# Around the last segment: unpaced loads, Gelus behind the last exponential, and a new order of the tail

## The chip, the cores and the metric

The kernel runs on one core of a Trainium2 chip. The metric is the device time of one execution in microseconds (us), as the median of several runs. The profile is one execution, taken by the hardware profiler; its times count from the start of its span.

## The reference

The reference is one transformer block over 2048 tokens of width 512. The attention part goes through the sequence in 64 segments of 32 tokens, one after the other, because 8 memory rows are handed from each segment to the next. The MLP part follows for all tokens.

```
mem = mem0                                   # 8 rows
for s in range(64):                          # x is layernormed first
    h = concat([mem, x[32 s : 32 s + 32]])   # 40 rows x 512
    q, k, v = h Wq, h Wk, h Wv               # 32 heads of 128
    p = softmax(mask(q k^T * 128**-0.5))
    o = (p v) Wo                             # 40 rows x 512
    mem = o[:8]; outs.append(o[8:])
h  = x + concat(outs)
h2 = h + gelu(layernorm(layernorm(h)) w1 + b1) w2 + b2    # 512 -> 1792 -> 512, tanh Gelu
```

## The kernel before, in words

**How the work is staged.** Of the eight rows that a segment hands on, the next segment needs the result at once; everything else of a segment may lag. The kernel therefore runs a chain of segments in which the tensor engine (PE) projects q, k and v for 24 own rows and 8 memory rows, multiplies scores and values for the memory rows, and applies Wo (`wo`, L1294). The ordinary rows' softmax (`sa_mm`, L1182, with the exponential at L1209) and their values (`pv_a`, L1236; its result leaves PSUM in `pv_a_ev`, L1257) follow one segment later. The last eight rows of each segment are handled for blocks of four segments, that is for 128 tokens, by `wo_B` (L1321) and `fold` (L1347), which queues its small adds on POOL. `nat` (L1354) turns a finished block of 128 output rows back by a transposing DMA (L1356), adds x (L1359), takes the layernorm statistics and writes the rows to `h_mid` in HBM (L1376).

**The MLP.** It works in four groups of 512 tokens. Group 0 is treated apart. Its w1 product is done during segments 56 to 63 in places where PE would have had gaps: `hx_early` (L1461) loads a block of `h_mid` into one of the buffers kq 4 and 5, VectorE (DVE) normalizes it in place (L1465), `hn_early` (L1468) transposes it by DMA, `w1_early` (L1454) loads slices of w1 and `w1_pair` (L1480) multiplies two of the 14 column blocks of w1 at a time (L1488). The products of the first six pairs are copied out of PSUM without Gelu into homes in buffers that are no longer used (`gT0_home`). ScalarE (ACT) holds the exponential's table until the last softmax, so that the Gelus of group 0 (`gelu`, L1473; its instructions are L1476) come at the end. The seventh pair is multiplied behind the last segment; its two Gelus read PSUM directly and are the first to run. The order in which group 0's w2 products (L1681) use the 14 blocks is `ORDER0` (L32): 12, 13, 0, 1, ... 11. The list `rest` (L1708) says which other work is put in front of which w2 step: `nat` of block 14, `pv_a` of segment 63, `wo_B` of block 15 with its folds, `wo` of "segment" 65 (the ordinary rows of segment 63) and `nat` of block 15. `wo(NS, ...)` (L1705) is the same for segment 62. The last four w2 steps run tile by tile (L1732), and DVE adds the residual out of PSUM (L1735) and the result is stored (L1737).

Groups 1 to 3 load their rows from `h_mid` (`p2_load`, L1420), normalize them on DVE (`p2_norm`, L1426), transpose them by DMA (`p2_T`, L1437), add b2 to the residual on POOL (`p2_res`, L1432), and then run w1 (L1674), Gelu (L1677) and w2 (L1681) with a lag of four blocks. The row buffer and the residual buffer have two halves; group 2 takes group 0's half, and so its load waits for `p2_res(0)`. The w2 loads (L1692, seven of 256 KB) and w1 loads (L1697, eight of 224 KB) go into the memory of Wk and are free to start when the last segment's k projection is done.

**What sets the order.** All operations are recorded with their data dependencies and planned durations, and PE's order is written out by hand (`ORDERS`, `ORDER_LAST`). `schedule` (L260) is a list scheduler: it takes operations by a key from `PLAN` or by their rank (the longest planned way to the end), and puts each at the earliest free place on its engine; where an operation may run on ACT or DVE (`either`, L206) it goes where it would end first. `lat` (L241) is the planned delay from one operation to a dependent one: 2.0 us behind a DMA, with exceptions. Each engine then runs its operations in that order and waits on semaphores; all DMAs of this part go through one in-order queue on the SP engine.

**Pacing.** PE's instructions are fetched in blocks of 256 (`FETCH_N`) by DMA. `windows` (L404) goes through the SP queue after planning, and from segment 2 on moves each DMA to a stretch between two planned fetches, by making it wait for a PE operation:

```
i = bisect.bisect_right(ends, t) - 1
o.start = max(t, ends[i])
if pe[i] not in o.deps:
    o.deps.append(pe[i])
```

Then `order` (L436) sorts every queue by start, so a DMA that was moved also gets a later place in the SP queue. The other engines' planned starts are not worked out again. `pads` and `pauses` shift PE's fetch points and add waits on PE near them.

Of the kernel before, what the change touches and what calls it, by code (L numbers as in the profile page):

```python
# [17 lines left out]
HOP = {"pe": 0.23, "act": 0.04, "dve": 0.04, "pool": 0.06, "sp": 2.0}  # L18
# [10 lines left out]
KEEP = True  # L29
WINDOWS, WIN_LO, WIN_HI, WIN_BEHIND = True, 1.0, -0.8, 0.4  # L30
PAUSES, PAUSE_IN, PAUSE_US = 3, 64, 0.5
ORDER0 = (12, 13, 0, 1, 2, 3, 4, 5, 6, 7, 8, 9, 10, 11)  # L32
HALVES = ("kq", "KA", "QT", "ZCm", "VS", "nmc", "EC", "rsc", "PC", "PTC", "OTm", "OTx", "KB", "QTB", "VSB", "W1o")
BONUS = {'TTS': -3.0, 'opB': -3.0, 'TTB': -3.0}
LEAN = 0.2
# [116 lines left out]
class Sched:  # L152
# [87 lines left out]
    @staticmethod  # L240
    def lat(p, o):  # L241
        if p.is_dma:
            return {"oN": 4.4, "xT": 3.6}.get(p.kind, HOP["sp"])
        if p.eng == "pe" and o.eng == "pe":
            return 0.0
        return HOP[p.eng] + (0.06 if o.eng == "pe" else 0.0)
# [157 lines left out]
    def windows(self):  # L404

        self.align()
        pe = self.streams["pe"]
        ends = [o.start + o.dur for o in pe]
        t0 = min(o.start for o in pe if o.tag is not None and o.tag[0] == 2)
        marks = [t for t, _ in self.marks if t > t0] + [1e9]  # L410
        used = [t + d for t, d in self.marks if t > t0] + [1e9]
        for o in self.streams["sp"]:
            early = o.start
            for d in o.deps:
                early = max(early, d.start + d.dur + self.lat(d, o))
            o.start = early
            if not o.is_dma or o.start < t0:
                continue
            late = min([d.start - o.dur - self.lat(o, d) for d in o.succ], default=1e9)
            size = o.span  # L420
            w = max(0, bisect.bisect_right(marks, early) - 1)
            while w < len(marks) - 1:
                t = max(early, used[w])
                if t + size <= marks[w + 1] + WIN_HI or t > late:
                    break
                w += 1
            if w >= len(marks) - 1 or t > late:
                continue
            used[w] = t + size
# [4 lines that stand above are left out]
        self.order()  # L434
# [212 lines left out]
ACTF = mybir.ActivationFunctionType  # L647
# [17 lines left out]
FC = F // P  # L665
NTOK = 2048
NS = NTOK // SEG
NTB = NTOK // P
# [48 lines left out]
def build_kernel(nc, A_x, A_mem0, A_Wq, A_Wk, A_Wv, A_Wo, B_w1, B_b1, B_w2, B_b2, out):  # L717
    scale = float(E) ** -0.5
    S = Sched(nc)
    st = contextlib.ExitStack()  # L720
    with st:
# [14 lines left out]
        xT = XX[:, 2, :].rearrange("p (c t) -> p c t", c=DC)  # L736
        hB = XX[:, 3, :].rearrange("p (b c t) -> p b c t", b=RBLK, c=DC)
        oN = sb("oN", [P, DC, P])
# [20 lines left out]
        EC = sb("EC", [P, 2, 64], F32)  # L759
# [3 lines left out]
        SA = sb("SA", [P, 8, LK], F32)  # L763
# [22 lines left out]
        b1t = sb("b1t", [P, FC], F32)  # L786
# [32 lines left out]
        for j in range(4):  # L819
            for b in range(2):  # L820
# [5 lines left out]
             reads=["maskL"], writes=["maskL"])  # L826
# [143 lines left out]
        def copy2(out, src, n, ps_=True, scale_=None):  # L970

            fast = 1.0 if ps_ else 0.5
            if scale_ is None:
                return {"act": (lambda e: e.copy(out, src), t_act(n, ps_)), "dve": (lambda e: e.tensor_copy(out, src), 0.155 + 1.0e-3 * n * fast)}  # L974
            return {"act": (lambda e: e.mul(out, src, scale_), t_act(n, ps_)),  # L975
                    "dve": (lambda e: e.tensor_scalar(out, src, scale_, None, ALU.mult), 0.155 + 1.0e-3 * n * fast)}
# [280 lines left out]
        def pv_a_ev(s):  # L1257
            bk, sg = s // 4, s % 4
            two, keys = pv_a_place(s)
            for t in range(2):  # L1260
                src = two[:, t, :].rearrange("p (k q) -> p k q", q=SEG)[:, :, 0:NA]
                S.either(copy2(OT[:, s % 2, 16 * t:16 * t + 16, 0:NA], src, 384), reads=[keys[t]], writes=[("OTx", s % 2, t)])
            src = two.rearrange("p t (k q) -> p t k q", q=SEG)[:, :, :, NA:SEG]
            ot = OTB[:, bk % 2, :, 8 * sg:8 * sg + 8].rearrange("p (t k) q -> p t k q", t=2)
            S.either(copy2(ot, src, 256), reads=keys, writes=[("OTB", bk % 2, sg)])
# [81 lines left out]
        def fold(n, after=()):  # L1347
            tag, S.tag = S.tag, None
            for f in folds[:n]:
                S.narrow(f(after))  # L1350
            del folds[:n]
            S.tag = tag
# [39 lines left out]
        SBT = TBS * P  # L1392
# [77 lines left out]
            S.dma(lambda e: e.dma_start_transpose(hnT0[:, :, t, :], kq[:, i].rearrange("p a e b -> p (a e b)")), 256, reads=[("kq", i)],  # L1470
                  writes=[("hnT", "first", t)] + hnT0_keys[t], after=after)

        def gelu(fc, src, reads, first):  # L1473
            p = fc // 2
            g = gT0_home[p][0][:, fc % 2, :]
            S.op("act", lambda e: e.activation(g, g if src is None else src, ACTF.Gelu_apprx_tanh, bias=b1t[:, fc:fc + 1], scale=1.0),  # L1476
                 reads=[("gT0", fc), "b1t"] + reads, writes=[("gT0", fc)] + (gT0_home[p][1] if reads else []), dur=0.65 + 1.1 * first,
                 after=[S.last_writer["SA"], S.last_writer[("EC", 1)]] + ([] if first else [S.last_writer[("gT0", ORDER0[0])]]))

        def w1_pair(p, banks, keep=True):  # L1480
            views, keys = homes[p]
            for cc in range(DC):
                v, c0, _ = [w for w in views if w[1] <= cc < w[2]][0]

                def f(e, v=v, c=cc - c0, cc=cc):
                    for n in range(2):
                        for j in range(4):
                            ins = e.matmul(ps[banks[n]][32 * j:32 * j + 32, 0:SBT], v[:, c, n * P + 32 * j:n * P + 32 * j + 32], hnT0[:, cc], start=(cc == 0), stop=(cc == DC - 1),  # L1488
                                           tile_position=(0, 32 * j), skip_group_check=True)
                    return ins  # L1490
                S.op("pe", f, reads=keys + [("W1p", p, c) for c in range(DC)] + [("hnT", "first", t) for t in range(TBS)], writes=[("ps", b) for b in banks],
                     dur=0.4315, mode=MC, ni=16)
            g, gkeys = gT0_home[p]
            for n in range(2):
                if keep:
                    S.either(copy2(g[:, n, :], ps[banks[n]][:, 0:SBT], SBT), reads=[("ps", banks[n])], writes=[("W1o", n), ("gT0", 2 * p + n)] + gkeys)
                else:
                    gelu(2 * p + n, ps[banks[n]][:, 0:SBT], [("ps", banks[n])], n == 0)

        def gT_of(k, fc):  # L1500
            return gT0_home[fc // 2][0][:, fc % 2, :] if k == 0 else gT[:, fc, :]
# [199 lines left out]
        p2_T(1)  # L1701

        early, later = (5, 6), 4
        w1_pair(NP - 1, early, False)
        wo(NS, later, mem=False)  # L1705
        for fc in range(FC - 2):
            gelu(fc, None, [], False)
        rest = {0: lambda: nat(NTB - 2), 3: lambda: (pv_a(NS - 1), pv_a_ev(NS - 1)), 5: lambda: (wo_B(NTB - 1, later), fold(14)), 7: lambda: (wo(NS + 1, 7, mem=False), nat(NTB - 1))}  # L1708
        p2_res(0)
        for n, fc in enumerate(ORDER0[:FC - 4]):  # L1710
            rest.get(n, lambda: None)()
# [82 lines left out]
```

## Time and profile before

| what | value |
| --- | --- |
| median of 3 runs | 803.06 us |
| the runs | 800.70, 804.13, 803.06 us |
| the profiled execution's own time | 802.49 us |
| its span | 800.8 us |
| mean granted PE clock in it | 0.994 |
| PE busy | 766.7 us |
| last segment's projections on PE end | about 692.8 us |
| group 0's w2 products start | 702.1 us |
| group 1's w1 products start | 722.5 us |

The profile is read as follows. PE, PEld, DVE, ACT, POOL and SPq are the matmuls, the weight loads, VectorE, ScalarE, GpSimd and the DMA queue of SP. A row of a timeline gives the start, the duration, the engine, the source line, the operation with its output and input buffers, the count, and in brackets the idle time of the engine before it with what ended that. MLP buffers lie in the memory of attention buffers and are shown under those names: WK is w1 and w2, WQ holds group 1 to 3's Gelu results and rows, WV the normalized rows, the residual and the output.

### The profile page before, as it was taken

What the parts mean: (1) busy time and instruction counts of PE and PEld (TensorE: products, weight loads), DVE (VectorE), ACT (ScalarE), POOL (GpSimd) and SP (SyncE); (2) the same over time, 40 slices, a digit from 0 to 9 for tenths busy, and PEclk for the clock granted to TensorE, in tenths of its full rate; (3) what the DMA queues carried; (4) which work ended last, traced back from release to release, by engine and by line L of the source; (5) the groups of instructions that cost most, each with busy time, mean ns of one, the idle gap of its engine ahead of it and who ended that gap; (6) DMA issues with size and microseconds to landing.
All of it is one profiled execution on the core that took longest, in us unless ns stands there. A gap on an engine that the chain in (4) does not pass through costs nothing.

```text
span 800.8 us, 45344 instructions
## 1 busy us (share of the span) xinstructions
PE 766.7 (96%) x19686; PEld 424.6 (53%) x20409; DVE 583.3 (73%) x1859; ACT 530.6 (66%) x1381; POOL 308.5 (39%) x831
## 2 busy tenths in 40 slices
PE   3789999999999999999999999999999999989998
PEld 1345455555655555555555555565655666533443
DVE  3258788888888888888888888888888787722211
ACT  2447777777677777677777777777676767643432
POOL 3013223434343444444444444444452425364300
PEclk9999999999999999999999999999999999999999
DMA  9950001010102010201010101010113101275200
GB/s 334 395 180 24 17 14 26 18 45 14 44 7 57 4 48 13 47 14 43 18 43 18 41 21 42 18 37 23 37 31 83 50 25 49 70 185 131 80 26 27
DMA packets 65056, 48.02 MB, mean 60 GB/s; under 512 B 28500, under 2 KB 61276, under 8 KB 64860
## 3 DMA queue, kind: packets, MB, share of 16 engines
q1 hardware_dynamic: 64528, 44.85, 19.5%
q8 instruction: 158, 2.59, 1.3%
q14 instruction: 38, 0.31, 0.1%
q10 hardware_dynamic: 332, 0.27, 0.1%
HBM read 31.08 MB, written 8.13 MB: 49 GB/s over the span
## 4 chain that ended last, share of the span: by engine, by line
PE 92%; DMA 3%; SPq 2%; ACT 2%; issue 1%; DVE 0%; DVEq 0%; ACTq 0%
PE high L956 34%; PE high L699 17%; PE quad L1286 15%; PE quad L1681 5%; PE high L1674 5%; PE high L1325 3%; SPq L859 2%; PE quad L1139 2%; DMA WQ<-in_A_Wq_dram 2%; PE quad L1196 2%; PE quad L1246 2%; PE high L1488 2%; PE quad L1170 1%; PE high L1170 1%; PE high L1286 1%
## 5 line engine op out<-in xcount | busy, mean ns | idle before, releaser
L956 PE MATMUL high<-WQ,hT 128*32 128x512 bf16 x1796 | 158.1, 383 | 1.3 <-DVE hT L1292 1.0
L699 PE MATMUL high<-WK,hT 128*32 128x512 bf16 x1260 | 127.0, 379 | 0.1
L1219 POOL TENSOR_TENSOR PA<-SA,rsa 128x256 bf16<-128x256 f32 x64 | 39.7, 620 | 219.6 <-DVE rsa L1211 131.1
L1286 PE MATMUL quad<-WO,OT 128*32 128x256 bf16 x4032 | 122.5, 273 | 0.7 <-issue 0.7
L956 PE MATMUL high<-WV,hT 128*32 128x512 bf16 x1528 | 115.7, 379 | 0.0
L975 ACT ACTIVATE kq<-high 128x512 bf16<-128x512 f32 x160 | 94.2, 598 | 22.0 <-PE high L956 18.6
L974 ACT CAST kq<-high 128x512 bf16<-128x512 f32 x161 | 93.8, 583 | 21.7 <-PE high L956 20.0
L1286 PEld LDWEIGHTS quad<-WO,OT 128*32 128x32 bf16 x4032 | 102.1, 97 | 6.4 <-issue 1.4
L1227 POOL COPY BD<-PTA 32x128 f32<-32x128 f32 x256 | 78.6, 307 | 16.3 <-DVE PTA L1223 0.6
L956 PEld LDWEIGHTS high<-WQ,hT 128*32 128x32 bf16 x1796 | 52.4, 95 | 56.0 <-issue 24.0
L997 DVE STREAM_TRANSPOSE KALL<-kq 128x256 f32<-128x256 f32 x160 | 69.4, 434 | 9.7 <-ACT kq L974 7.0
L974 ACT CAST VS<-high 128x512 bf16<-128x512 f32 x126 | 73.2, 581 | 0.1
L954 PEld LDWEIGHTS <-hT 128*32 128x32 bf16 x3248 | 52.6, 96 | 35.4 <-DVE hT L1292 7.9
L1677 ACT ACTIVATE WQ<-high,b1t 128x512 bf16<-128x512 f32 x42 | 28.9, 687 | 55.8 <-PE high L1674 55.8
L974 ACT CAST OT<-quad 128x384 bf16<-128x384 f32 (+1 forms) x126 | 47.3, 375 | 24.3 <-PE quad L1174 23.2
L1298 DVE STREAM_TRANSPOSE TT<-quad 128x256 f32<-128x256 f32 x63 | 28.4, 450 | 42.7 <-PE quad L1286 42.5
L1033 ACT COPY KALL<-KALL 128x128 f32<-128x128 f32 x63 | 18.8, 298 | 59.2 <-PE quad L1196 59.0
L997 DVE STREAM_TRANSPOSE QT<-kq 128x256 f32<-128x256 f32 x128 | 54.5, 426 | 1.6 <-ACT kq L975 1.3
L956 PE MATMUL high<-WK,hT 128*32 128x512 bf16 x788 | 55.2, 379 | 0.0
L1338 POOL TENSOR_TENSOR opT<-TTB,TTS 32x64 bf16<-32x64 f32 x128 | 40.3, 315 | 35.9 <-DVE opT L1292 20.0
L699 PE MATMUL high<-WV,hT 128*32 128x512 bf16 x520 | 53.2, 379 | 0.0
L1139 PEld LDWEIGHTS quad<-KALL,ZC 128*32 128x32 bf16 x1984 | 31.0, 96 | 41.6 <-POOL BD L1227 17.8
(187 smaller groups left out, 1612.0 us busy)
## 6 DMA issues: line engine op xcount, KB each, us to landing
WV<-in_A_Wv_dram SPq DMA_DIRECT2D x4, 1024.0 KB, 10.2
WK<-in_A_Wk_dram SPq DMA_DIRECT2D x4, 1024.0 KB, 18.6
WQ<-in_A_Wq_dram SPq DMA_DIRECT2D x4, 1024.0 KB, 17.6
WO<-in_A_Wo_dram SPq DMA_DIRECT2D x16, 256.0 KB, 7.5
v_last<-VSB SPq DMA_DIRECT2D x60, 64.0 KB, 2.4
VBD<-v_last SPq DMA_DIRECT2D x60, 64.0 KB, 2.0
h_mid<-xr SPq DMA_DIRECT2D x16, 128.0 KB, 1.9
WQ<-h_mid SPq DMA_DIRECT2D x4, 512.0 KB, 4.5
```

What stands on the lines that cost most here:

```text
L699: return e.add_instruction(mybir.InstMatmult(name="I-%d" % (4000000 + _kept[0]), engine=mybir.EngineType.PE, start_tensor_calc=start, stop ...
L954: e.ldweights(l, tile_position=(0, 32 * j))
L956: ins = e.matmul(o, l, m, start=(k == 0), stop=(k == DC - 1), tile_position=(0, 32 * j), skip_group_check=True)
L974: return {"act": (lambda e: e.copy(out, src), t_act(n, ps_)), "dve": (lambda e: e.tensor_copy(out, src), 0.155 + 1.0e-3 * n * fast)}
L975: return {"act": (lambda e: e.mul(out, src, scale_), t_act(n, ps_)), "dve": (lambda e: e.tensor_scalar(out, src, scale_, None, ALU.mult), ...
L997: S.op("dve", lambda e: e.transpose(out, src), reads=[("kq", i)], writes=[key], dur=t_dve(256) + 0.02)
L1139: ins = e.matmul(o[32 * j:32 * j + 32, :], zc_window(h), rhs, start=False, stop=(i == 3), tile_position=(0, 32 * j), skip_group_check=True)
L1227: S.narrow(S.op("pool", lambda e, j=j, rows=rows: e.tensor_copy(words(BD[rows, par, :, j, :, :]), words(PTA[rows, 0:4])), reads=["PTA"], w ...
L1286: ins = e.matmul(ps[bank][32 * j:32 * j + 32, 0:256], lhs(slot(h)), wo_cols(h, b), start=(k == 0), stop=(k == 15), tile_position=(0, 32 * ...
L1338: return e.tensor_tensor(o[32 * q:32 * q + 32, c:c + 2], x, y, ALU.add)
L1674: ins = e.matmul(ps[bank][:, 0:SBT], W1[:, cc, fc * P:(fc + 1) * P], hnT_of(k)[:, cc, :], start=(cc == 0), stop=(cc == DC - 1))
L1681: S.op("pe", lambda e: e.matmul(quad[:, t, c0:c0 + w], gT_of(k, fc)[:, t * P:(t + 1) * P], W2[:, fc, c0:c0 + w], start=(fc == (0 if k else ...
```

## The change

Five edits are made. `windows` leaves DMAs alone whose planned start lies at or behind the first PE operation of the last segment (`t1`). The planned latency behind the early row loads into kq 4 and kq 5 is 4.0 us, not 2.0. The seventh w1 pair is copied out of PSUM like the others, on ACT or DVE, and all 14 Gelus run in place, in the order 0 to 13; each waits for the last exponentials, and all but the first also for the first. `ORDER0`, and with it the order of the w2 loads and products, is 0 to 13. In the tail, the Gelus are recorded ahead of `wo(NS, ...)`, and three of the entries of `rest` come two w2 steps earlier.

```diff
-ORDER0 = (12, 13, 0, 1, 2, 3, 4, 5, 6, 7, 8, 9, 10, 11)
+ORDER0 = tuple(range(14))
...
         if p.is_dma:
-            return {"oN": 4.4, "xT": 3.6}.get(p.kind, HOP["sp"])
+            return {"oN": 4.4, "xT": 3.6, "kq4": 4.0, "kq5": 4.0}.get(p.kind, HOP["sp"])
...
         t0 = min(o.start for o in pe if o.tag is not None and o.tag[0] == 2)
+        t1 = min(o.start for o in pe if o.tag is not None and o.tag[0] == NS - 1)
...
-            if not o.is_dma or o.start < t0:
+            if not o.is_dma or not t0 <= o.start < t1:
                 continue
...
-        def gelu(fc, src, reads, first):
-            p = fc // 2
-            g = gT0_home[p][0][:, fc % 2, :]
-            S.op("act", lambda e: e.activation(g, g if src is None else src, ACTF.Gelu_apprx_tanh, bias=b1t[:, fc:fc + 1], scale=1.0),
-                 reads=[("gT0", fc), "b1t"] + reads, writes=[("gT0", fc)] + (gT0_home[p][1] if reads else []), dur=0.65 + 1.1 * first,
-                 after=[S.last_writer["SA"], S.last_writer[("EC", 1)]] + ([] if first else [S.last_writer[("gT0", ORDER0[0])]]))
-
-        def w1_pair(p, banks, keep=True):
+        def gelu(fc):
+            g = gT0_home[fc // 2][0][:, fc % 2, :]
+            S.op("act", lambda e: e.activation(g, g, ACTF.Gelu_apprx_tanh, bias=b1t[:, fc:fc + 1], scale=1.0), reads=[("gT0", fc), "b1t"], writes=[("gT0", fc)],
+                 dur=0.65 + 1.1 * (fc == 0), after=[S.last_writer["SA"], S.last_writer[("EC", 1)]] + ([S.last_writer[("gT0", 0)]] if fc else []))
+
+        def w1_pair(p, banks):
...
             for n in range(2):
-                if keep:
-                    S.either(copy2(g[:, n, :], ps[banks[n]][:, 0:SBT], SBT), reads=[("ps", banks[n])], writes=[("W1o", n), ("gT0", 2 * p + n)] + gkeys)
-                else:
-                    gelu(2 * p + n, ps[banks[n]][:, 0:SBT], [("ps", banks[n])], n == 0)
+                S.either(copy2(g[:, n, :], ps[banks[n]][:, 0:SBT], SBT), reads=[("ps", banks[n])], writes=[("W1o", n), ("gT0", 2 * p + n)] + gkeys)
...
         early, later = (5, 6), 4
-        w1_pair(NP - 1, early, False)
+        w1_pair(NP - 1, early)
+        for fc in range(FC):
+            gelu(fc)
         wo(NS, later, mem=False)
-        for fc in range(FC - 2):
-            gelu(fc, None, [], False)
-        rest = {0: lambda: nat(NTB - 2), 3: lambda: (pv_a(NS - 1), pv_a_ev(NS - 1)), 5: lambda: (wo_B(NTB - 1, later), fold(14)), 7: lambda: (wo(NS + 1, 7, mem=False), nat(NTB - 1))}
+        rest = {0: lambda: nat(NTB - 2), 1: lambda: (pv_a(NS - 1), pv_a_ev(NS - 1)), 3: lambda: (wo_B(NTB - 1, later), fold(14)), 5: lambda: (wo(NS + 1, 7, mem=False), nat(NTB - 1))}
```

## The prediction

> **What bounds the kernel now.** I read the page first, then who waited for whom from 560 us to the end, then each engine in order of time around 690 to 725 us, where the edited code runs, and last the stretch around 612 us, which one edited constant reaches.
>
> ```profile
> span 800.8 us, 45344 instructions
> PE 766.7 (96%) x19686; PEld 424.6 (53%) x20409; DVE 583.3 (73%) x1859; ACT 530.6 (66%) x1381; POOL 308.5 (39%) x831
> ```
>
> PE is busy 96% of the span. No edit removes a matmul, so all that the change can give is PE's waiting time and matmuls run at a lowered clock. The answer on waits from 560 us on says how much there is in reach:
>
> ```profile
> PE high L1674 <- DMA WQ<-WV: 3.6, 1, 3.6
> PE quad L1681 <- ACT QTB L1476: 1.4, 1, 1.4
> PE high L1170 <- DVE PTC L1156: 1.1, 1, 1.1
> ```
>
> PE in order of time (start, duration, operation, idle before it) shows where the tail's waits stand:
>
> ```profile
> 698.80 1.92 PE L1286 MATMUL high<-WO,OT 128*32 128x256 bf16 x64
> 702.13 1.67 PE L1681 MATMUL quad<-WK,QTB 128*128 128x512 bf16 x7 [1.41 <-ACT QTB L1476]
> 704.60 0.41 PE L1246 MATMUL high<-BD,VS 64*128 64x64 bf16 x16
> 706.23 1.02 PE L1681 MATMUL quad<-WK,VSB 128*128 128x512 bf16 x4 [0.18 <-DMA WK<-in_B_w_dram]
> 707.18 1.91 PE L1325 MATMUL high<-WO,OTB 128*32 128x512 bf16 x32
> 709.25 0.81 PE L1681 MATMUL quad<-WK,VSB 128*128 128x512 bf16 x3 [0.16 <-ACT VBD L1476]
> 722.51 2.77 PE L1674 MATMUL high<-WQ,WK 128*128 128x512 bf16 x7 [3.57 <-DMA WQ<-WV]
> ```
>
> The last row is the big one: group 0's second matrix product is done at 722.51 - 3.57 = 718.94, and group 1's first waits for the transposes of its normalized rows. That wait also costs clock. Rows of stretches (PE, PEld, DVE, ACT, POOL busy, then clock, DMA share, GB/s) and two pieces of the critical chain:
>
> ```profile
> 690.00:700.00 10.00, 10.00 (x280) 6.15 (x264) 7.52 (x21) 5.42 (x11) 4.32 (x12) 1.00 0.37 122
> 720.00:730.00 10.00, 7.44 (x26) 2.98 (x28) 4.37 (x10) 3.44 (x5) 3.59 (x9) 0.83 0.74 189
> 43.00:48.00 5.00, 4.38 (x106) 2.85 (x108) 2.45 (x8) 2.04 (x6) 0.00 (x0) 0.66 1.08 345
> ```
> ```profile
> 722.51 6.25 PE high L1674 x20
> 772.97 4.50 PE high L1674 x20
> ```
>
> The same first twenty W1 products take 6.25 us behind the wait and 4.50 us in group 3, where PE came in without one: 1.75 us lost to a clock of 0.83 over that stretch.
>
> **The part on the load queue (no pacing behind the last segment).** Why were the transposes late? The DMA queue on SP runs in order:
>
> ```profile
> 692.40 0.47 SPq L1420 DMA_DIRECT2D WQ<-h_mid  x1
> 699.75 1.84 SPq L1437 DMA_TRANSPOSE WQ<-WV  x1
> 704.64 0.47 SPq L1420 DMA_DIRECT2D WQ<-h_mid  x1
> 708.87 1.40 SPq L1356 DMA_TRANSPOSE oN<-opT  x1
> 716.49 0.35 SPq L1420 DMA_DIRECT2D WQ<-h_mid  x1
> 716.88 3.81 SPq L1437 DMA_TRANSPOSE WQ<-WV  x3
> ```
> ```profile
> SPq L1420 <- POOL WV L1432: 6.2, 1, 6.2
> SPq L1692 <- PE high L1325: 4.0, 1, 4.0
> SPq L1437 <- PE quad L1681: 2.1, 2, 1.3
> ```
> ```profile
> 698.23 1.50 DVE L1426 TENSOR_SCALAR WV<-WQ,agg,rst 128x512 bf16<-128x512 bf16 x4
> 720.94 0.41 DVE L1426 TENSOR_SCALAR WV<-WQ,agg,rst 128x512 bf16<-128x512 bf16 x1 [2.53 <-DMA WQ<-h_mid]
> 721.27 2.48 DVE L1735 TENSOR_TENSOR WV<-quad,WV 128x512 bf16<-128x512 f32 x4
> ```
> ```profile
> 711.98 4.48 POOL L1432 TENSOR_TENSOR WV<-WQ 128x512 f32<-128x512 bf16 x4 [5.10 <-DMA WQ<-h_mid]
> ```
>
> All four normalized blocks are in place at 698.23 + 1.50 = 699.73, yet only one transpose is issued then. The other three were moved by the pacing to windows tied to W2 products (waits for L1681), and so landed in the in-order queue behind the load for group 2 (L1420 at 716.49), which itself waits 6.2 us until POOL is done with its buffer at 711.98 + 4.48 = 716.46. Without pacing they stand in the queue where their data is ready. The dependency that remains is real: load of group 1's rows, normalization, transposes. The load is now queued behind several W2 loads of 256 KB instead of one; at the 0.37 DMA share of 690 to 700 us there is room, and I allow it 1 to 2 us. Then four transposes at 1.27 (3.81 / 3) to 1.84 us of queue time are issued by 701.7 + 4 x 1.84 = 709.1 at the latest. In the row above the last of three was issued by 720.69 and PE started at 722.51, 1.8 us later; so they are in place by about 711, and PE wants them at 717.2 (below). The W1 loads behind them in the queue, eight of 224 KB, are the cover's next edge: four of them are needed at 717.2, and from 709 on at 254 GB/s, the rate of the congested 705 to 715 us below, their 0.9 MB takes 3.5 us. So the wait of 3.57 us and the clock loss of 1.75 us both go. The 0.18 us wait for a W2 load goes too, as all W2 loads are issued before 699.
>
> **The part on the Gelus.**
>
> ```profile
> 694.94 0.48 ACT L1209 ACTIVATE SA<-SA 128x320 f32<-128x320 f32 x1
> 695.33 0.37 ACT L974 CAST OTB<-quad 128x256 bf16<-128x256 f32 x1
> 699.07 1.28 ACT L1476 ACT_TABLE_LOAD   x1 [3.37 <-PE high L1488]
> 707.79 1.32 ACT L1476 ACTIVATE VBD<-VBD,b1t 128x512 bf16<-128x512 bf16 x2
> ```
>
> ACT stands idle 3.37 us until the last W1 pair is in PSUM, because that pair's two Gelus came first, and PE's first W2 product waits for them. In the changed order Gelu 0 needs only the last exponential. ACT is free at 695.70, so the table load ends at 697.0 and Gelu 0 (half of 1.32) at about 697.7, three microseconds before PE asks for it (698.80 + 1.92 = 700.72). Load and 14 Gelus took 699.07 to 709.11, 10.04 us; from 695.70 they end at 705.7. The edit adds two copies of 128x512 out of PSUM for the last pair, of about 0.58 us each by the page's row for such copies:
>
> ```profile
> L974 ACT CAST VS<-high 128x512 bf16<-128x512 f32 x126 | 73.2, 581 | 0.1
> ```
>
> If both fall on ACT the last Gelu ends at 706.9, and it is wanted in the last quarter of the W2 products, after 713. Cost zero; cover 6 us. The waits of 1.41 and 0.16 us go. The probability-value product of the last segment moves two W2 steps forward but stays two steps ahead of the WO product that needs its result, so that distance is as before, and so is that to the last WO product; it needs one of the two banks that the new copies free, about 699.7, and runs at 701.6.
>
> PE's new end of group 0: work from 702.13 to 718.94 is 16.81 us with 0.34 us of the waits that go, so 16.47 us; 700.72 + 16.47 = 717.2 against 718.94, and group 1 starts there instead of at 722.51.
>
> **The part on the planned latency (kq4, kq5 at 4.0).** From 600 to 620 us:
>
> ```profile
> DVE kq L1465 <- DMA kq<-h_mid: 1.8, 2, 1.2
> ```
>
> DVE stood in front of two early loads for 1.8 us; PE's 1.1 us wait for PTC is behind that. Planned 2 us later the normalizations find their data, and 1.1 us goes. They also occupy another 0.4 us slot on DVE; at 73% busy I take nothing for it, with 0.4 lost as the other bound.
>
> **What is late next.** Group 0's results leave PSUM by the four adds of 721.27 to 723.75, which stand behind a normalization of group 2 that waits for its load (2.53 us). PE asks for the first of the four banks after twenty W1 products, at 717.2 + 4.5 = 721.7, and for the last at 722.3. PE's earlier end lets the add for bank 0 go ahead of that normalization; the other three then end at 721.35 + 3 x 0.62 = 723.2 if the load lands as now, 0.9 us too late, and in time if the chain from group 0's row load on (POOL starts at 711.98) is a microsecond sooner. I take 0.5 us, in the middle; bounds 0, and 1.5 with all four adds where they are now (723.75).
>
> Instruction fetch is the other unknown. PE fetches its program by the same DMA engines, and the loads now come in one lump. The DMA answers for 690 to 700 and 705 to 715 us:
>
> ```profile
> q8 instruction: 2, 0.03, 1.4%
> ```
> ```profile
> DMA packets 2331, 2.54 MB, mean 254 GB/s; under 512 B 665, under 2 KB 2201, under 8 KB 2329
> q1 hardware_dynamic: 2329, 2.52, 97.4%
> q8 instruction: 1, 0.02, 0.6%
> ```
>
> One fetch inside a stretch with the engines 97.4% busy left a gap of at most 0.2 us on PE there; two fetches now fall into the lump. I take 0.4 us, bounds 0 and 2 x 2.
>
> **The sum**, against the profiled execution's own time, 802.49 us (span 800.8 and 1.69 around it; the median of the three runs is 803.06, so this one is 0.57 below): 1.41 + 0.18 + 0.16 + 3.57 + 1.75 + 1.10 = 8.17 gone, 0.5 + 0.4 new, 7.27 net: 795.2 us.
>
> Two rules of the Trainium skill bear on this. "TensorE: Matmul & The Clock Gate" (Part 1) says that the clock halves after an idle window of about 3.4 us and returns after about 3.4 us of work; that fits 720 to 730 us and would make the clock term 3.4 / 2 = 1.7 for 1.75, an estimate from that page. But the row 43 to 48 us shows 0.66 with PE busy 4.38 of 5 us, so the trace asks for less idleness than the rule. "DMA: Bandwidth & Descriptors" (Queues, rings and completion order) says each DMA engine takes turns between queues packet by packet, by which a fetch would not stand behind all queued loads; the single fetch at 97.4% agrees, and by that rule the slower rival below is nearly excluded.
>
> **The rivals.** (1) The adds bind (18%): group 0's row load, now queued behind four transposes, lands 1.5 us later than before, the adds end at 725.3 and PE loses 3.0 us in place of 0.5: 797.7, or 799.4 with the clock halved after it. For it: the transposes take up to 1.84 us of the queue each. Against: its competitors of 705 to 715 us have been moved earlier. (2) The transposes stay late (10%): something else in the in-order queue, such as the oN transpose that waits for POOL or the load that waits for 716.46, still stands ahead of them. Then PE comes 1.75 us sooner and waits longer, and only the 1.10 us stays: 802.49 - 1.10 = 801.4. Against: the transposes' data are ready at 699.73, at least seven microseconds before either of these. (3) Slower (6%): each of the two fetches in 692 to 702 us waits for the load queue to drain. PE goes through 544 instructions in 690 to 700 us, two fetches' worth, so it has under 5 us in hand per fetch; with 2.4 MB queued (seven W2 loads, the row load of 512 KB, b2 of 128) at 254 GB/s, 9.4 us, each stalls PE for 4 us and then costs 1.75 us of clock: 795.2 + 11.5 = 806.7. It beats the gain once a stall with its clock passes 3.6 us. Against: the fetch under 97.4% load. (4) The change does nothing at 612 us or disturbs the plan of the last ten segments (4%): 796.3 to 798.
>
> **How the numbers follow.** Forecast 62%, 795.2: from 793.0 (no new waits gives 794.3, and two of the three runs lie over 1 us from the median) to 797. With rivals 1 and 4 the range reaches 799; rivals 2 and 3 and the tails are outside. 0.5%, 4.0 us, is about what a measurement of this kernel can tell from no change: faster means under 799.0. Forecast, rivals 1 and 4 give 0.81 (some of rival 1's tail goes to no change), rival 2 and that tail 0.13, rival 3 0.06.
>
> **What would show it.** The gap before the first L1674 at or under 0.3 us and clock 1.00 through 715 to 730 us; three or four L1437 transposes issued before 710; the table load near 695.7 and no wait of L1681 for ACT; no wait of L1465 for its load and none of 1.1 us near 612. I am wrong if PE waits at L1674 for a transpose or W1, at L1681 for an add by over 2 us, or if "issue" gaps appear on PE between 692 and 705.

## The result, and the profile after

The changed kernel takes 798.61 us (median of four runs, 797.54 to 799.39) against 803.15 us for the kernel before, run beside it (four runs, 800.70 to 804.13). The ratio is 0.9947, with a 95% interval of 0.9922 to 0.9972. Timed twice more, on other occasions, it gave 0.9931 (0.9909 to 0.9953) and 0.9959 (0.9942 to 0.9976). So it is faster, by about 4 to 5.5 us between the medians of an occasion; the forecast had 7.3 us.

The profiled execution took 797.54 us. The top of its page:

```profile
span 795.8 us, 45330 instructions
PE 765.4 (96%) x19686; PEld 424.7 (53%) x20409; DVE 585.3 (74%) x1862; ACT 530.0 (67%) x1380; POOL 308.1 (39%) x831
```

The span is 5.0 us shorter, PE's busy time 1.3 us. So more of the gain is waiting that went than clock that came back. These are PE's new waits (engine, tile and line, what ended the wait, total, times, longest):

```profile
PE high L1487 <- DMA VSB<-in_B_w_dram: 1.7, 1, 1.7
...
PE high L1287 <- issue: 0.8, 1, 0.8
...
PE high L1326 <- DVE OTB L975: 0.7, 1, 0.7
...
PE high L1247 <- DVE QTB L975: 0.2, 1, 0.2
```

(Lines of the changed kernel are one higher than before's up to the Gelus, which are L1476 in both; its w1 products of groups 1 to 3 are L1670, its w2 products L1677, the residual adds L1731, the w2 loads L1688. In e2 and e6 all lines shown are one higher than before's.) The waits of 3.6 us for a transpose, of 1.4 us for a Gelu and of 1.1 us for PTC are gone. Four others stand in their place. PE in order of time:

```profile
700.11 1.49 PE L1287 MATMUL high<-WO,OT 128*32 128x256 bf16 x47 [0.80 <-issue]
...
702.75 0.41 PE L1247 MATMUL high<-BD,VS 64*128 64x64 bf16 x16 [0.18 <-DVE QTB L975]
...
705.79 1.91 PE L1326 MATMUL high<-WO,OTB 128*32 128x512 bf16 x32 [0.74 <-DVE OTB L975]
...
719.11 4.66 PE L1670 MATMUL high<-WQ,WK 128*128 128x512 bf16 x19
```

Group 1 starts at 719.11 without a wait, and its first products take 4.66 us, where they took 6.25. The stretch of 720 to 730 us, which had PE busy for 7.44 us at clock 0.83, is now:

```profile
720.00:730.00 10.00, 9.95 (x46) 4.23 (x46) 6.43 (x16) 5.50 (x8) 7.45 (x17) 1.00 0.54 148
```

On the SP queue the four transposes are issued one behind the other as soon as their rows are normalized, but the row load (L1421) now stands behind five w2 loads:

```profile
691.13 2.43 SPq L1688 DMA_DIRECT2D WK<-in_B_w_dram  x5
693.60 0.46 SPq L1421 DMA_DIRECT2D WQ<-h_mid  x1
...
700.99 5.93 SPq L1438 DMA_TRANSPOSE WQ<-WV  x4
```

ACT starts its Gelus right behind the last exponential and is done with them at 705.35:

```profile
695.23 1.28 ACT L1476 ACT_TABLE_LOAD   x1
...
704.03 1.32 ACT L1476 ACTIVATE QTB<-QTB,b1t 128x512 bf16<-128x512 bf16 x2
```

DVE shows where the new waits come from: it stands still for 2.42 us in front of group 1's normalization, and behind that come both new copies out of PSUM (QTB) and the casts of the values (OT, OTB), for which PE waits:

```profile
700.54 1.46 DVE L1427 TENSOR_SCALAR WV<-WQ,agg,rst 128x512 bf16<-128x512 bf16 x4 [2.42 <-DMA WQ<-h_mid]
701.93 1.41 DVE L975 CAST QTB<-high 128x512 bf16<-128x512 f32 x2
...
705.31 0.42 DVE L975 CAST OTB<-high 128x256 bf16<-128x256 f32 x1
...
721.01 2.44 DVE L1731 TENSOR_TENSOR WV<-quad,WV 128x512 bf16<-128x512 f32 x4
```

For the comparisons below each profile is cut at three marks on PE: the first ordinary-row score product of segment 53 and of segment 63, and the first w1 product of group 1. "After the mark" means after that of segment 63. "Tail" is the sum of the last two stretches. (The expectation of e8 calls the first mark segment 54. The traces hold 64 groups of these products, one for each of the segments 0 to 63, and the one at 592.65 us is the eleventh from the end, that of segment 53.)

| profile of | to segment 53 | 53 to 63 | 63 to group 1 | group 1 to end | tail | median us | ratio to before, 95% |
| --- | --- | --- | --- | --- | --- | --- | --- |
| before | 592.65 | 100.62 | 29.24 | 78.29 | 107.53 | 803.15 | |
| changed kernel | 593.39 | 99.67 | 26.05 | 76.69 | 102.74 | 798.61 | 0.9947 (0.9922 to 0.9972) |
| after_again | 593.26 | 100.24 | 26.01 | 76.99 | 103.00 | 798.28 | 0.9931 (0.9909 to 0.9953) |
| after_third | 593.17 | 100.86 | 26.06 | 76.61 | 102.67 | 797.63 | 0.9959 (0.9942 to 0.9976) |
| e1_paced | 592.24 | 101.26 | 28.69 | 76.71 | 105.40 | 802.02 | 1.0028 (1.0007 to 1.0048) |
| e2_only_unpaced | 594.67 | 100.21 | 25.16 | 81.86 | 107.02 | 801.11 | 1.0001 (0.9981 to 1.0021) |
| e3_lat2 | 593.59 | 99.33 | 26.14 | 76.64 | 102.78 | 797.27 | 0.9958 (0.9936 to 0.9980) |
| e4_rows_first | 594.77 | 99.36 | 26.50 | 76.77 | 103.27 | 798.93 | 0.9975 (0.9952 to 0.9998) |
| e5_norms_behind | 594.91 | 101.87 | 24.07 | 76.55 | 100.62 | 796.94 | 0.9925 (0.9903 to 0.9948) |
| e6_unpaced_adds_first | 594.41 | 100.41 | 25.15 | 77.43 | 102.58 | 798.63 | 0.9941 (0.9920 to 0.9962) |
| e7_w2_paced | 594.60 | 99.14 | 26.95 | 76.61 | 103.56 | 797.99 | 0.9932 (0.9912 to 0.9953) |
| e8_norms_lat2 | 592.19 | 99.77 | 24.84 | 76.60 | 101.44 | 795.31 | 0.9931 (0.9907 to 0.9956) |

The three profiles of the changed kernel show how to read the table. Their stretch from segment 53 to 63 differs by 1.2 us, the tail by 0.3 us. What happens in the tail is therefore judged by the tail's columns, a result for the whole kernel by the ratios. The medians belong to four occasions, on which the kernel before had 803.15 (changed kernel), 801.08 (e1 to e4), 803.83 (after_again, e5 to e7) and 801.39 us (after_third, e8); only ratios are compared across them.

### The profile page after: what moved, and what is told of

It reads as the page before. It is cut to its first block, busy times and chain, and to the rows that moved or that the text cites. A ratio compares the mean times of both kernels' runs of the same rounds, so it can differ in the third digit from the quotient of the medians.

```text
span 795.8 us, 45330 instructions
## 1 busy us (share of the span) xinstructions
PE 765.4 (96%) x19686; PEld 424.7 (53%) x20409; DVE 585.3 (74%) x1862; ACT 530.0 (67%) x1380; POOL 308.1 (39%) x831
## 4 chain that ended last, share of the span: by engine, by line
PE 90%; SPq 5%; DMA 2%; DVE 1%; issue 1%; ACT 0%; DVEq 0%
PE high L957 33%; PE high L700 17%; PE quad L1287 15%; PE quad L1677 6%; PE high L1670 5%; PE high L1326 3%; SPq L860 2%; SPq L878 2%; PE quad L1140 2%; PE quad L1197 2%; PE quad L1247 2%; PE quad L1171 1%; PE high L1171 1%; PE high L1487 1%; DMA WO<-in_A_Wo_dram 1%; DMA WQ<-h_mid 1%
## 5 line engine op out<-in xcount | busy, mean ns | idle before, releaser
L975 ACT CAST OT<-quad 128x384 bf16<-128x384 f32 (+1 forms) x126 | 47.3, 375 | 26.3 <-PE quad L1175 25.2
```

## The experiments

**e1_paced: the Gelus and the new order alone.** The changed kernel with the pacing kept to the end:

```diff
-        t1 = min(o.start for o in pe if o.tag is not None and o.tag[0] == NS - 1)
+        t1 = 1e9
```

> The changed kernel with the pacing kept behind the last segment, so that the Gelu, order and latency edits stand alone. My theory: unpacing alone removed the wait for the transposes, and it also made the new waits of the tail (0.80 us 'issue' inside the WO product near 699, 0.18 and 0.74 us for DVE's copies, which stand behind the late row load). So here the wait of about 3.5 us before group 1 and the halved clock behind it are back, the three tail waits are gone, and the w1-slice wait of 1.7 us near 622 stays: about 798.6 + 5.3 - 1.7 = 802.2 us. Rival: the tail waits come from the Gelu and order edits themselves; then they are still there and the time is about 804.

Measured: 802.02 us, 1.0028 (1.0007 to 1.0048). PE waits for a transpose in front of group 1 as in the kernel before, for 2.54 us; two of four transposes are again issued late, at 717:

```profile
722.19 4.66 PE L1670 MATMUL high<-WQ,WK 128*128 128x512 bf16 x20 [2.54 <-DMA WQ<-WV]
```
```profile
716.70 0.34 SPq L1421 DMA_DIRECT2D WQ<-h_mid  x1
717.08 2.50 SPq L1438 DMA_TRANSPOSE WQ<-WV  x2
```

The twenty products behind that wait take 4.66 us, as behind no wait. The pacing is thus what holds the transposes. The waits for DVE and the 'issue' gap are gone, as expected; between 713 and 717 us PE waits for paced w2 loads instead, 1.61 us in three pieces. The profile's tail is 2.1 us shorter than before's, but the median isn't: this profiled execution (800.58 us) lies 1.4 us under its median, and before's (802.49) 1.4 us above the median of this occasion. How far the tail of the one profile stands for the other executions stays open here; by the ratio, whose interval lies just above 1, these edits alone bring nothing and may cost a little.

**e2_only_unpaced: the pacing alone.** The kernel before with the two edited lines of `windows` and nothing else:

```diff
+        t1 = min(o.start for o in pe if o.tag is not None and o.tag[0] == NS - 1)
...
-            if not o.is_dma or o.start < t0:
+            if not o.is_dma or not t0 <= o.start < t1:
```

> The kernel before with only the loads behind the last segment unpaced. My theory: the wait for the transposes (3.57 us) and the clock loss (1.75) go, the wait for the Gelus (1.41) and the 1.1 us near 612 stay, and the instruction fetch stalls by about 0.8 us as in the changed kernel: 803.15 - 5.3 + 0.8 = 798.6 us, the same as the changed kernel, since the other edits gave nothing net. Rival: the other edits do contribute; then this is about 800 us or more.

Measured: 801.11 us, 1.0001 (0.9981 to 1.0021): nothing gained, where 798.6 was expected, although group 1 starts 25.16 us after the mark, even sooner than in the changed kernel. The time is lost again behind it. DVE, then PE:

```profile
725.75 0.61 DVE L1427 TENSOR_SCALAR WV<-WQ,agg,rst 128x512 bf16<-128x512 bf16 x1 [3.48 <-DMA WQ<-h_mid]
726.28 2.47 DVE L1736 TENSOR_TENSOR WV<-quad,WV 128x512 bf16<-128x512 f32 x4
```
```profile
727.02 0.39 PE L1682 MATMUL quad<-WK,WQ 128*128 128x512 bf16 x1 [2.32 <-DVE WV L1736]
...
728.81 0.61 PE L1682 MATMUL quad<-WK,WQ 128*128 128x512 bf16 x1 [0.21 <-DVE WV L1736]
```
```profile
720.00:730.00 10.00, 7.05 (x27) 2.33 (x26) 6.34 (x16) 3.44 (x5) 7.84 (x18) 0.94 0.39 115
730.00:740.00 10.00, 10.00 (x43) 4.35 (x42) 1.79 (x6) 3.44 (x5) 1.70 (x4) 0.89 0.37 84
```

The adds that empty group 0's four banks (L1736) stand behind one block of group 2's normalization (L1427), which waits 3.48 us for its rows. PE wants the first bank after its twenty w1 products, at 724.70, and gets it at 727.02. This is the prediction's rival 1, in the half of the change where the planner left the adds where they were.

**e6_unpaced_adds_first: the same, with the adds ahead.** To e2 is added that group 2's normalization depends on the last add of group 0:

```diff
-                    p2_norm(k + 1)
+                    p2_norm(k + 1, [S.last_writer[("ob", 0, 3, 0)]] if k == 1 else [])
```

(`p2_norm` hands the second argument on as a further dependency.)

> The kernel before, unpaced behind the last segment as in the run that only did that, and with group 2's first normalization put behind the four adds on DVE. In that run the time did not move: PE no longer waited for the transposes, but waited 3.6 us in five pieces for the adds, and the clock was below 1.00 from 720 to 740 us. My theory: those adds were late only because on DVE they stood behind the normalization that waits for group 2's row load, so here that wait and the clock loss go and the time is about 5 us below the kernel before, 0.994 of it. Rival: the adds are held by POOL's residual sums or the oN transpose; then PE still waits there and the time stays within 2 us of the kernel before.

Measured: 798.63 us, 0.9941 (0.9920 to 0.9962), as much as the whole change. The stretch behind group 1's start falls from 81.86 to 77.43 us:

```profile
722.46 2.48 DVE L1736 TENSOR_TENSOR WV<-quad,WV 128x512 bf16<-128x512 f32 x4
...
726.31 1.59 DVE L1427 TENSOR_SCALAR WV<-WQ,agg,rst 128x512 bf16<-128x512 bf16 x4 [0.61 <-DMA WQ<-h_mid]
```
```profile
720.00:730.00 10.00, 9.95 (x46) 4.22 (x46) 7.11 (x16) 4.96 (x8) 8.16 (x18) 1.00 0.53 145
```

So e2's loss is the order on DVE, shown by changing only that. In the changed kernel the adds come ahead of that normalization as well (721.01 against 725.60), without an edit that asks for it: the planner arrives at that order with the other edits. Nothing holds it there; in e4 the adds stand behind the normalization again (723.38 against 721.87).

e2 and e6 show one thing more. Their PE still waits for a Gelu, up to 1.04 us, and group 1 nevertheless starts 25.2 us after the mark, 0.9 us sooner than in the changed kernel. As planned there, the edits other than the unpacing cost more ahead of group 1 than they gain.

**e3_lat2: the latency entries.** The changed kernel without `"kq4": 4.0, "kq5": 4.0`.

> The changed kernel with the planned latency of the early row loads back at 2.0 us. My theory: the latency edit took away the 1.1 us wait near 612 and brought the 1.7 us wait for a w1 slice near 622; here the first is back and the second gone, so about 0.6 us faster than the changed kernel: 798.0 us, and the tail from the last segment on as in the changed kernel. Rival: the wait near 622 comes from elsewhere and stays; then about 799.7 us.

Measured: 797.27 us, 0.9958 (0.9936 to 0.9980), against 0.9947 (0.9922 to 0.9972) of the changed kernel on another occasion: the entries carry nothing that can be measured. The trace says why. Without them PE waits near 612 us for PTC, in this kernel's row:

```profile
612.38 0.26 PE L1171 MATMUL high<-PTC,VS 64*128 64x16 bf16 x8 [0.58 <-DVE PTC L1157]
```

With them that wait is gone in all seven profiles, but in four of the seven PE waits ten microseconds later for a slice of w1; in the changed kernel's first profile:

```profile
621.89 1.05 PE L1487 MATMUL high<-XX,VSB 128*32 128x512 bf16 x16 [1.66 <-DMA VSB<-in_B_w_dram]
```

The slices share the SP queue with the transposes of the rows normalized later. In the changed kernel:

```profile
616.73 1.20 SPq L1471 DMA_TRANSPOSE XX<-kq  x1
617.97 0.58 SPq L1459 DMA_DIRECT2D VSB<-in_B_w_dram  x1
```

The last of the four VSB slices starts at 617.97; in the kernel before, two together start at 615.21. Over the five profiles with 2.0 (before, e2, e3, e6, e8) the wait for PTC is 1.10, 0.79, 0.58, 1.02 and 0.63, mean 0.82; over the seven with 4.0 the wait for the slice is 1.66, none, 1.32, 1.57, none, 1.27, none (changed kernel, after_again, after_third, e1, e4, e5, e7), mean 0.83. One wait was exchanged for another of the same mean size. That the transposes ahead of the slice make it late is argued from their order in the queue; no run moves them alone.

**e4_rows_first: the row load ahead of the w2 loads.** The changed kernel with `p2_load(1)` recorded ahead of them, and each of them held behind it:

```diff
+        p2_load(1)
+        rows1 = S.dmas[-1]
...
-            S.dma(lambda e, f=f: e.dma_start(W2[:, f], w2_d[:, f]), 256, writes=[("W2", i)], after=used["WK"])
-        p2_load(1)
+            S.dma(lambda e, f=f: e.dma_start(W2[:, f], w2_d[:, f]), 256, writes=[("W2", i)], after=used["WK"], behind=rows1)
```

> The changed kernel with group 1's row load put ahead of all w2 loads in the queue. My theory: DVE's normalizations then find their rows at about 698 us in place of 700.5, the copies out of the two banks and the value casts behind them come sooner, and PE's waits of 0.18 and 0.74 us go; the 'issue' stall of 0.8 us stays; group 0 ends 0.9 us sooner. If nothing else holds group 1, 797.7 us. Rival: group 1 is then held by the adds out of PSUM, which stand behind the oN transpose and POOL's residual (both wait for loads near 716 to 719 us); then a wait of up to 1 us appears at group 1's first w2 product and the time stays at 798.6.

Measured: 798.93 us, 0.9975 (0.9952 to 0.9998); group 1 starts 26.50 us after the mark, no sooner. The planner, knowing the rows to be early, put the normalizations ahead of work for segment 63 on DVE, and PE waited for what DVE did behind them:

```profile
702.07 1.93 PE L1287 MATMUL high<-WO,OT 128*32 128x256 bf16 x64 [2.24 <-DVE TTB L1330]
```

This run doesn't answer the question that it was made for, whether the late row load costs time; e5 does.

**after_again: the changed kernel unchanged**, to see how steady its waits are.

> The changed kernel itself once more, beside the kernel before on the chip that also times the other runs of this set: about 0.994 of the kernel before, with PE's waits of the tail (0.8 us 'issue' near 699, 0.2 and 0.7 us for DVE) again within a few tenths.

Measured: 798.28 us, 0.9931 (0.9909 to 0.9953). The waits are not steady: the gap of 0.80 us isn't there, and group 1 still starts 26.01 us after the mark, since PE then stood longer in front of the product that waits for the copies:

```profile
703.15 0.41 PE L1247 MATMUL high<-BD,VS 64*128 64x64 bf16 x16 [1.24 <-DVE QTB L975]
...
706.19 1.91 PE L1326 MATMUL high<-WO,OTB 128*32 128x512 bf16 x32 [0.73 <-DVE OTB L975]
```

**e5_norms_behind: group 1's normalization behind the last value cast.** The changed kernel with e6's edit, and with group 1's normalization and transposes recorded behind the last of segment 63's casts and made to depend on it:

```diff
-        p2_norm(1)
-        p2_T(1)
...
-        rest = {0: lambda: nat(NTB - 2), 1: lambda: (pv_a(NS - 1), pv_a_ev(NS - 1)), 3: lambda: (wo_B(NTB - 1, later), fold(14)), 5: lambda: (wo(NS + 1, 7, mem=False), nat(NTB - 1))}
+        rest = {0: lambda: nat(NTB - 2), 1: lambda: (pv_a(NS - 1), pv_a_ev(NS - 1), p2_norm(1, [S.last_writer[("OTB", 1, 3)]]), p2_T(1)), 3: lambda: (wo_B(NTB - 1, later), fold(14)), 5: lambda: (wo(NS + 1, 7, mem=False), nat(NTB - 1))}
```

> The changed kernel with DVE's order mended by two added dependencies: group 1's normalizations behind the last value cast, and group 2's first normalization behind the four adds. My theory (DVE is held in order by a normalization whose row load is late, and the casts behind it hold PE): the waits of 0.2 and 0.7 us go, group 0 ends 0.9 us sooner counted from segment 63's score product, and since the adds no longer stand behind a load for group 2 either, the rest keeps its 76.7 us: 0.9 us faster than the changed kernel. Rival: group 1's transposes, now issued about 4 us later, or the adds (held by POOL's residual) come too late, and the 0.9 us turns up as a wait at group 1's start or at its first w2 products.

Measured: 796.94 us, 0.9925 (0.9903 to 0.9948). DVE no longer stands still for the rows, and neither wait of PE is left; group 1 starts 24.07 us after the mark, 2 us sooner than in the changed kernel:

```profile
702.54 1.42 DVE L975 CAST QTB<-high 128x512 bf16<-128x512 f32 x2 [0.70 <-PE high L1487]
...
706.87 0.42 DVE L975 CAST OTB<-high 128x256 bf16<-128x256 f32 x1
707.40 1.38 DVE L1427 TENSOR_SCALAR WV<-WQ,agg,rst 128x512 bf16<-128x512 bf16 x4
```

The normalization starts 3 us behind the landing of its rows (704.33 in the trace), and 3 us later after the mark than in the changed kernel, and costs nothing: the stretch from group 1 on is 76.55 us, so the rival falls. (This edit also moves group 0's row load, from 709.38 to 702.35 us on the SP queue, ahead of the transposes.) The whole kernel's gain over after_again doesn't show in the ratios: their intervals overlap, and this profile's first two stretches are the longest of the table.

**e7_w2_paced: all but the first two w2 loads paced again**, so that fewer bytes lie around the row load.

```diff
-            if not o.is_dma or not t0 <= o.start < t1:
+            if not o.is_dma or not t0 <= o.start < (1e9 if o.kind == "W2" and o.writes[0][1] > 1 else t1):
```

> The changed kernel with the third to seventh w2 loads paced again, so that about 1.3 MB less is queued between 692 and 700 us. My theory: the 0.8 us 'issue' gap in the WO product near 699 is an instruction fetch delayed by the lump of loads; here it is gone (under 0.2), and the row load of group 1 lands about 3 us sooner, so the 0.2 and 0.7 us waits for DVE go as well; against that one or two w2 steps wait for their load, up to 1.5 us together. About 0 to 1 us faster than the changed kernel. Rival: the gap is a property of the instruction stream's position and stays at 0.8 us.

Measured: 797.99 us, 0.9932 (0.9912 to 0.9953). The gap and the two waits for DVE are gone, and waits for w2 itself, three of together 2.56 us where up to 1.5 was expected, took their place; group 1 starts 26.95 us after the mark:

```profile
712.95 1.89 PE L1677 MATMUL quad<-WK,hT 128*128 128x512 bf16 x8 [0.32 <-DMA WK<-in_B_w_dram]
...
716.39 0.59 PE L1677 MATMUL quad<-WK,VBD 128*128 128x512 bf16 x2 [1.55 <-DMA WK<-in_B_w_dram]
717.67 0.59 PE L1677 MATMUL quad<-WK,QTB 128*128 128x512 bf16 x2 [0.69 <-DMA WK<-in_B_w_dram]
```

**e8_norms_lat2 and after_third: the best of these, timed beside the changed kernel.** e8 is e5 without the latency entries.

> Changed kernel with group 1's normalization recorded behind the last value cast (as in the run e5_norms_behind) and the two latency entries taken out. My theory: the normalizations no longer hold PE between 700 and 707 us, so group 1 starts 24.0 to 24.3 us after segment 63's score product, against 26.0 in the changed kernel, and the rest of the tail is as there, 76.5 to 77; the latency entries carry nothing. So 1.5 to 2 us under the changed kernel on the same chip: a ratio to the kernel before near 0.991. Rival A: what PE gains before group 1 it loses again behind it, since the transposes then land later than PE wants them: group 1 starts at 24 but the tail behind it grows by 1.5 us or more, and the medians of the two kernels agree within 0.5 us. Rival B: the latency entries do carry something before 693 us: this kernel is then no faster than the changed one although its tail is 2 us shorter, and the stretch from segment 54 to segment 63 is over 101.5 us.

> The changed kernel unchanged, timed beside e8_norms_lat2 on the same chip. My theory: 798.0 to 798.6 us, ratio 0.993 to 0.995, group 1 starting 26.0 us after segment 63's score product, with one or both of the two waits of PE for DVE between 700 and 707 us. Rival A of that run expects the same here.

Measured: e8 795.31 us (794.25 to 798.41, six runs), 0.9931 (0.9907 to 0.9956); the changed kernel beside it 797.63 us (796.36 to 800.34, eleven runs), 0.9959 (0.9942 to 0.9976). e8 beats the kernel before; its median is 2.3 us under the changed kernel's, but the two intervals overlap. In the profiles its tail is 1.23 us shorter (101.44 against 102.67), not the 1.5 to 2 us expected, and all of that lies ahead of group 1, so the rival by which it is lost again behind group 1 falls. The part that is missing is in this row:

```profile
698.86 1.49 PE L1287 MATMUL high<-WO,OT 128*32 128x256 bf16 x47 [0.65 <-issue]
```

The changed kernel's median and ratio lie just outside what was expected of them (798.0 to 798.6 us, 0.993 to 0.995); its waits for DVE are there, 0.83 and 0.73 us. In e8, with DVE's waits gone, nothing hides the gap any more: 24.84 is e5's 24.07 with 0.65 added and 0.12 left.

## Why the prediction was right, and where it failed

The direction and the two large steps held, and the time lies in the range; the predicted 795.2 us was too low by 3.4. Split by the stretches of the two profiles, the forecast's 7.27 us were 4.91 ahead of group 1 (5.31 from the earlier start, less 0.4 for fetches), 1.25 behind it (clock 1.75, adds 0.5) and 1.10 near 612 us. Measured were 3.19, 1.60 and 0.21 (the first two stretches together), 5.00 in all. Of the 1.72 us that are missing ahead of group 1, 0.92 are waits for DVE, 0.40 are the 'issue' gap beyond what was allowed for fetches, and 0.38 were never there (third point below).

- **Transposes and clock: right.** No wait in front of L1670, clock 1.00, four transposes issued by 706.92 (forecast 709.1 at the latest). The first twenty products, 19 of them recorded, take 4.66 us, so 1.59 us came back. That is all of the loss: the row of the timeline before gives 4.66 us for group 3's twenty as well, and the 4.50 behind the forecast's 1.75 is a piece of the chain, which starts 0.16 us later. e1 shows that the pacing held the transposes.
- **Gelus and w2 loads: right.** The table load started at 695.23 (forecast 695.70), the last Gelu ended at 705.35 (705.7), and no w2 product waited for either.
- **"1.41 + ... + 0.16" gone: 0.38 us too much.** Group 0's w2 products are 56 (14 blocks times four row tiles), but the trace before holds 53 of them. The rows at 702.13 (x7 for 8) and 709.25 (x3 for 4) each lack a first product of 0.22 us. So PE's wait for the Gelu was about 1.2 us, and the 0.16 us were no wait. The changed kernel's profile has a gap of 0.16 us at the same place, and after_third, which holds all 56 products, has none there. The rows of the changed kernel and of after_third:

```profile
707.86 0.81 PE L1677 MATMUL quad<-WK,VSB 128*128 128x512 bf16 x3 [0.16 <-issue]
```
```profile
708.61 1.04 PE L1677 MATMUL quad<-WK,VSB 128*128 128x512 bf16 x4
```

- **"Cost zero; cover 6 us" and "it needs one of the two banks that the new copies free, about 699.7": the step that failed.** The cover was worked out for the Gelus. The copies were costed on ACT alone; the planner put both on DVE, where they are in order behind group 1's normalization, and that behind its row load. PE doesn't need the Gelus early, but it needs the banks, for segment 63's probability-value product, and then the casts behind them. PE's waits for them sum to 0.92, 1.97 and 1.56 us in the three profiles of the changed kernel. e5 shows that this order is the cause: with the normalization behind the casts both waits go, and group 1 starts 24.07 us after the mark. The forecast, without its 0.4 for fetches, had 23.9, or 24.3 without the 0.38 us.
- **The row load, "1 to 2 us" later: mis-sized, and followed down one path only.** From issue to landing it took 4.6 us in the kernel before and 6.9 us in the changed one, and it was issued 1.2 us later, so it came 3.5 us later. The prediction carried its lateness to the transposes, where there was room, and not to what else DVE had queued behind the normalization.
- **Adds, 0.5 us: none, by luck.** The prediction asked for group 0's row load to come a microsecond sooner. It came 4.4 us later, and so did the residual that POOL makes of it for the adds (716.41 here, 711.98 before):

```profile
716.41 4.66 POOL L1433 TENSOR_TENSOR WV<-WQ 128x512 f32<-128x512 bf16 x4 [7.29 <-DMA WQ<-h_mid]
```

What saved it is that the planner put all four adds ahead of group 2's normalization, where the prediction had expected only the first. DVE ends them at 723.45 and PE asks for the first bank at 723.60; no profile of the changed kernel shows a wait there. "Bounds 0, and 1.5" held. Rival 1's mechanism was real: e2 is it, at the cost of the whole gain.

- **Fetch, 0.4 us: a gap of 0.80 us, which cost nothing.** The prediction had named such an 'issue' gap as a sign of being wrong. It lies ahead of DVE's waits, and where it is missing (after_again) they are longer, 1.97 us for 0.92, and group 1 starts just as late (26.01 and 26.05 us after the mark). Without this cover it costs its length (e8). That it is a fetch is argued from its place: the gap ends at the same product, the one with 47 left of 64, in five of the nine profiles with unpaced w2 loads (0.80, 0.17, 0.25, 0.35 and 0.65 us in the changed kernel, after_third, e3, e6 and e8) and in none of the three with paced ones. The rival with stalls of 4 us each didn't come. "DMA: Bandwidth & Descriptors" of the Trainium skill (Queues, rings and completion order) says that a DMA engine takes turns between its queues packet by packet; gaps of at most 0.80 us, with the DMA engines busy for 0.60 to 0.88 of 690 to 700 us in those five, agree, if they are fetches.
- **Latency entries, "1.1 us goes": failed.** It went, and a wait of the same mean size came for a w1 slice. The prediction looked for the cost on DVE, where the normalizations run, and not on the SP queue, where their transposes stand ahead of that slice.

What stays open: the time up to segment 63 differs by 1.0 us between the three profiles of the changed kernel, and by up to 3.7 us between kernels that are edited only behind it, and e1's median doesn't show the gain of its profile's tail. No run here tells why.

## What to carry to other kernels

When an edit makes a load later, follow everything that stands in order behind the instruction that waits for it, on its engine, and not only the data that it makes: the work behind may be wanted sooner than the result. Two edits can each be worth nothing and together the whole gain, if the first moves the wait to a place that only the second clears; so try each alone before calling one of them useless. And a gap that lies ahead of a longer wait costs nothing until that wait is mended.

## What the runs showed of the hardware

- **The clock.** Single waits of 2.24 us (e4) and 2.54 us (e1) were followed by full speed, the one of 3.57 us (before) wasn't. In e2 a wait of 2.32 us and three of 0.21 us, with single products between, did lower it, to 0.94 over 720 to 730 us and 0.89 over 730 to 740 us. "TensorE: Matmul & The Clock Gate" of the Trainium skill (Part 1) puts the drop behind an idle window of about 3.4 us. e1 and e4 agree; in e2 the idle time sums to 2.95 us within 4.11 us (724.70 to 728.81), so here less than a wholly idle window was enough.
- **One load among others.** The same 512 KB took 4.6 us to land with the DMA engines busy for 0.37 of 690 to 700 us, and 6.9 us with 0.79:

```profile
WQ<-h_mid SPq DMA_DIRECT2D x1, 512.0 KB, 4.6
```
```profile
WQ<-h_mid SPq DMA_DIRECT2D x1, 512.0 KB, 6.9
```

The first row is of the kernel before, the second of the changed one (size, and the time from issue to landing). In the eight profiles with five w2 loads issued just ahead of it the load takes 6.6 to 7.7 us. In e4, where it is issued ahead of them, it takes 4.4 us although the engines are busy for 0.83 of 690 to 700 us: so what stands ahead of the load matters more here than how busy the engines are.
